# First attention scores of seven batches in 64x32 tiles on TensorE, later due times for weight chunks, and a new order

## The chip, the cores and the metric

The kernel runs on one core of a Trainium2 chip. The core has a matrix engine (TensorE, PE in the profile, with PEld for its weight loads), a vector engine (VectorE, DVE), a scalar engine (ScalarE, ACT), GpSimd (POOL), which here issues the loads, and SyncE (SP), which here issues the stores. The metric is the device time of one execution in microseconds, as the median of several runs.

## The reference

Two stages follow each other. For 8 batches of 8 heads, 576 tokens and head size 64, an attention with 32 packed queries `p` runs in both directions; then a two-layer MLP with squared ReLU is applied to the tokens.

```python
p_packed = sm_attn(p, k, v)            # 32 rows per head: softmax(p k^T / 8) v
out = sm_attn(q, p_packed, p_packed)   # 576 rows per head: softmax(q pp^T / 8) pp
x = out.transpose(0, 2, 1, 3).reshape(4608, 512)
h = x @ w_in                           # 512 x 2048
return (np.maximum(h, 0) ** 2) @ w_out # 2048 x 512
```

## The kernel before

The eight heads of a batch are two quads of four heads; a quad fills 128 partitions (4 heads x 32 dimension pairs of k, or 4 heads x 32 packed queries). Per batch the steps are as follows, with the names that the planner uses.

- **Tk, Tq**: VectorE transposes a quad of k or q (lines 437 and 434) into `kT` and `qT`. The two halves of the head size, `dh` 0 and 1, lie interleaved in the last axis, so that an operand for one half takes every second bf16 element.
- **S1**: the first scores, 128 rows (4 heads x 32 packed queries) by 576 tokens for one quad (line 440, `s1`). The stationary operand `pT_bd` is block-diagonal: 128x128 with one 32x32 block for each head and zeros elsewhere. For each quad there are two matmuls of 512 columns (L446, one for each `dh`) and two of 64 columns (L448), all over the whole 128x128 array, accumulated in a pair of PSUM banks. VectorE takes the row maximum (L452), ScalarE the exponential (L456), after which the pair of banks is free; VectorE normalizes (L462, L463).
- **E, PV, XT**: the probabilities are transposed on TensorE (L469), multiplied with v (L484, column tiles of 64), and the packed outputs are spread out for the next steps (L496).
- **M**: the packed outputs times `w_in`, so that the first MLP layer becomes a product of the second attention's probabilities with a matrix `M` of 128 rows for each quad (L516). These matmuls are 64x32 tiles: eight tiles stand in the array at once. For batch 0 there are eight half steps, one for each quad and each 512-column chunk of `w_in`, for the others two steps of 16 matmuls.
- **S2, C, N**: the second scores (L536, L547, L554), their softmax on VectorE and ScalarE (L566 to L589), and the transposes (L598, L600).
- **F1**: `M` times the probabilities (L613), ReLU on ScalarE (L651), square on VectorE (L661). For batch 0 the tokens are split in a first part FA (256 tokens) and the rest (L626, L635, L642, L644).
- **F2**: the second MLP layer, 16 matmuls of 128x512 for each tile of 128 tokens (L669), the last tile in two halves (L686), then a copy out of PSUM (L356, L358) and the stores.

PSUM has eight banks. Banks 0 to 3 form two pairs (`ps_101`, `ps_102`), used by S1, M, S2 and F1; banks 4 and 5 (`pb_103`, `pb_104`) serve the smaller steps, 6 and 7 (`pb_105`, `pb_106`) F2.

The order of the instructions on every engine is made while the program is built, by a planner (`Plan`). It takes the steps as parallel streams with durations, dependences, due times and PSUM banks, and lets the ready step with the lowest priority value go next; the priorities come from a table of offsets (`TABLE`), one number for each step. A change of the tiling mode on TensorE is charged with `TURN`, 0.098 us in the plan. Loads are issued by GpSimd in the order of their priorities, at most eight at a time; a load counts as landed `LAG` after its own duration. Where the planner sees a gap on TensorE before the first F2 step, it puts in matmuls on zeros (L342) that keep the clock up. On the chip every engine simply executes its own list in order and waits on semaphores.

The lines that matter for what follows are `s1_steps` (one step `S1.b.qd` for each quad, then `E.b.qd`), `tr_steps` (k of the next batch may be transposed once both S1 steps of this batch are done), `load_wi` (the `w_in` chunks), `pv` (which reads the columns of one head in `e1`), and `TABLE`.

Of the kernel before, what the change touches and what calls it, by code (L numbers as in the profile page):

```python
# [8 lines left out]
ACT = mybir.ActivationFunctionType  # L9
# [5 lines left out]
P = 128  # L15
D = 64
NP = 32
QH = 4
JT = 18
GM = 4  # L20
# [33 lines left out]
class Plan:  # L54
# [193 lines left out]
TABLE = {'o': {'P.0': -351.91, 'X.0': -35.89, 'P.2': -372.52, 'X.1': -167.76, 'La0': -651.21, 'La1': -506.79, 'La2':  # L248
# [43 lines left out]


def kernel_impl(tc, q, k, v, p, w_in, w_out, out):
    nc = tc.nc
    B, H, S, Dh = q.shape
    assert Dh == D and S == JT * 32 and H == 2 * QH
    NQD = H // QH
    DMODEL, DFF = w_in.shape
    NE = w_out.shape[1]  # L300
    NFB = DFF // FB
    NWC = DFF // WCH
    HALF = S // 2
    TOK = B * S
    NT = TOK // P
    NKQ, NV, NR = 15, 5, 6
    VX = JT // 2
    TOKH = (2 * P, S - 2 * P)

    with ExitStack() as ctx:  # L310
# [110 lines left out]
        class Att:  # L421
# [53 lines left out]
            def pv(self, qd, u):  # L475
# [3 lines left out]
                for pr in range(2):  # L479
                    c0 = (2 * qd + pr) * NP  # L480
                    for g in range(GM + 1):
                        for e in range(2):
                            h = 2 * pr + e
# [523 lines left out]
```

## Time and profile before

| | us |
|---|---|
| median of 3 runs | 258.02 (257.89 to 258.48) |
| the profiled execution | 258.35 |
| its span | 256.6 |
| PE busy | 246.0 (96%) |
| DVE busy | 174.9 (68%) |
| ACT busy | 166.8 (65%) |
| granted TensorE clock | 1.0 |
| chain that ended last: share of PE | 88% |

The busy time of PE is a union of matmuls that overlap in the pipeline: a single matmul shows its latency (0.38 us for 512 columns), while the next one starts 0.22 us later. What a step costs on a full PE is therefore read as the distance from its first matmul to the first matmul of the step behind it, not as its duration.

### The profile page before, as it was taken

To read this page: it belongs to the slowest core of one execution; us is meant where nothing else is said; L and a number is where in the kernel's file an instruction comes from. 1 tells how busy PE (TensorE), PEld (TensorE's weight loads), DVE (VectorE), ACT (ScalarE), POOL (GpSimd) and SP (SyncE) were. 2 spreads that over 40 slices of the span, in tenths; PEclk is the share of its full clock that TensorE was granted. 3 is DMA by queue.
4 is the path that set the end of the run, shared out by engine and by line. 5 is a ranking of instruction groups with operands and counts; after the bars stand their busy time and mean duration, and the time that the engine had idled before them with its cause. 6 is when DMAs were issued, how large, how long until landed. Compare 5 with 4: busy or idle time off the path is not lost.

```text
span 256.6 us, 5483 instructions
## 1 busy us (share of the span) xinstructions
PE 246.0 (96%) x2142; PEld 143.7 (56%) x2175; DVE 174.9 (68%) x346; ACT 166.8 (65%) x282; POOL 43.3 (17%) x76
## 2 busy tenths in 40 slices
PE   7889999999999999999999999999999999999994
PEld 5556565466545664475446575466544665466542
DVE  7778858877897669966687868567839467657100
ACT  6436999688845796479864477589461685788001
POOL 8745544432424300000000000000000000000000
PEclk9999999999999999999999999999999999999999
DMA  6999999999999999310112020310130211111132
GB/s 112 191 206 204 202 197 209 209 245 233 206 222 228 237 206 191 86 45 0 43 41 74 24 72 0 84 41 0 46 81 19 66 43 31 51 43 39 43 92 74
DMA packets 26617, 28.47 MB, mean 111 GB/s; under 512 B 5472, under 2 KB 18016, under 8 KB 26592
## 3 DMA queue, kind: packets, MB, share of 16 engines
q0 software_dynamic: 18960, 18.55, 44.0%
q1 hardware_dynamic: 7008, 9.38, 13.4%
q8 instruction: 17, 0.28, 0.4%
q10 hardware_dynamic: 624, 0.20, 0.3%
q14 instruction: 8, 0.07, 0.1%
HBM read 37.22 MB, written 9.44 MB: 182 GB/s over the span
## 4 chain that ended last, share of the span: by engine, by line
PE 88%; DVE 6%; issue 1%; ACT 1%; DMA 1%; DVEq 0%; ACTq 0%
PE pb L669 46%; PE ps L613 22%; PE ps L536 3%; PE ps L446 3%; PE pb L484 2%; PE ps L626 2%; PE ps L516 2%; PE pb L516 2%; PE pb L469 1%; PE pb L598 1%; PE pb L686 1%; PE pb L342 1%; DVE M L358 1%; DMA p_f<-in_p_dram 1%; DVE kT L437 1%
## 5 line engine op out<-in xcount | busy, mean ns | idle before, releaser
L669 PE MATMUL pb<-w_out_b,gT 128*128 128x512 bf16 x530 | 139.7, 379 | 1.5 <-issue 0.6
L651 ACT ACTIVATE r<-ps 128x576 bf16<-128x576 f32 x112 | 71.8, 653 | 17.5 <-PE ps L613 13.5
L669 PEld LDWEIGHTS <-gT 128*128 128x128 bf16 x560 | 51.8, 98 | 51.8 <-issue 3.8
L613 PE MATMUL ps<-a,M 128*128 128x288 bf16 x448 | 71.5, 286 | 0.5 <-issue 0.2
L661 DVE TENSOR_TENSOR gT<-r 128x576 bf16<-128x576 bf16 x112 | 50.8, 457 | 29.5 <-ACT r L651 28.8
L613 PEld LDWEIGHTS <-M 128*128 128x128 bf16 x448 | 43.2, 98 | 21.4 <-issue 2.2
L358 DVE COPY o_sb<-pb 128x512 f32<-128x512 f32 (+1 forms) x22 | 14.6, 664 | 13.2 <-PE pb L669 8.7
L456 ACT ACTIVATE e1x<-ps,n 128x576 bf16<-128x576 f32 x16 | 11.8, 739 | 17.1 <-DVE n L452 16.5
L356 ACT COPY o_sb<-pb 128x512 f32<-128x512 f32 (+1 forms) x15 | 8.5, 573 | 19.4 <-PE pb L669 18.2
L356 ACT CAST M<-ps 128x1024 bf16<-128x1024 f32 (+1 forms) x15 | 14.7, 983 | 5.7 <-PE ps L516 5.7
L356 ACT CAST M<-pb 128x512 bf16<-128x512 f32 x29 | 15.9, 599 | 2.4 <-PE pb L516 2.4
L577 ACT ACTIVATE e<-d 128x1152 bf16<-128x1152 f32 (+2 forms) x10 | 9.7, 972 | 8.7 <-DVE d L571 8.6
L342 PE MATMUL pb<-zero 128*128 128x256 bf16 x87 | 13.8, 308 | 1.1 <-DVE zero L361 1.1
L411 POOL DMA_DIRECT2D v_b<-in_v_dram x16 | 11.2, 702 | 13.6 <-DMA k_b<-in_k_dram 8.8
L434 DVE STREAM_TRANSPOSE qT<-q_b 128x576 f32<-128x576 f32 x16 | 11.8, 760 | 1.7 <-DMA q_b<-in_q_dram 1.7
L583 DVE TENSOR_REDUCE t<-e 128x36 f32<-128x1152 bf16 (+2 forms) x10 | 11.0, 1096 | 2.5 <-ACT e L577 2.5
L406 POOL DMA_DIRECT2D q_b<-in_q_dram x16 | 8.9, 562 | 19.9 <-DVE kT L437 7.6
L452 DVE TENSOR_REDUCE n<-ps 128x1 f32<-128x576 f32 x16 | 11.6, 743 | 0.8 <-PE ps L448 0.7
L437 DVE STREAM_TRANSPOSE kT<-k_b 128x576 f32<-128x576 f32 x16 | 11.8, 759 | 0.3 <-DMA k_b<-in_k_dram 0.3
L589 DVE TENSOR_TENSOR n<-e,r 128x1152 bf16<-128x1152 bf16 (+2 forms) x10 | 11.1, 1107 | 0.1
L356 ACT COPY e<-pb 128x640 bf16<-128x640 bf16 x12 | 8.0, 702 | 4.7 <-PE pb L469 4.6
L342 PEld LDWEIGHTS <-zero 128*128 128x128 bf16 x87 | 8.8, 110 | 3.7 <-DVE zero L361 1.1
(75 smaller groups left out, 238.6 us busy)
## 6 DMA issues: line engine op xcount, KB each, us to landing
out_dram<-o_sb SPq DMA_DIRECT2D x140, 64.0 KB, 1.7
k_b<-in_k_dram POOLq DMA_DIRECT2D x16, 288.0 KB, 11.8
q_b<-in_q_dram POOLq DMA_DIRECT2D x16, 288.0 KB, 11.3
v_b<-in_v_dram POOLq DMA_DIRECT2D x8, 320.0 KB, 11.9
v_b<-in_v_dram POOLq DMA_DIRECT2D x8, 256.0 KB, 11.6
w_in_b<-in_moe_w_in_dram POOLq DMA_DIRECT2D x8, 256.0 KB, 10.3
w_out_b<-in_moe_w_out_dram POOLq DMA_DIRECT2D x8, 256.0 KB, 10.3
p_b<-in_p_dram POOLq DMA_DIRECT2D x1, 192.0 KB, 10.6
```

The costliest lines, as they stand in the source:

```text
L342: nc.tensor.matmul(half(7)[:, :2 * P], lhsT=zero[:, :P], rhs=zero, start=True, stop=True)
L356: nc.scalar.copy(dst, src)
L358: eng.tensor_copy(dst, src)
L411: nc.gpsimd.dma_start(self.v[64 * i:64 * i + 64, :, :n * D], src[:, :, i * GM * D:(i * GM + n) * D])
L434: nc.vector.transpose(self.qT[:, qd].rearrange("p s x -> p (s x)").bitcast(F32), self.t.q[qd][:].bitcast(F32))
L437: nc.vector.transpose(kT[:, qd].rearrange("p s x -> p (s x)").bitcast(F32).rearrange("p (x a j2) -> p j2 x a", a=32, j2=2), self.t.k[qd][: ...
L452: nc.vector.tensor_reduce(self.n1[:, qd:qd + 1], self.ps1[qd], axis=AX.X, op=ALU.max, negate=True)
L456: nc.scalar.activation(e1x[:, qd], self.ps1[qd], ACT.Exp, bias=self.n1[:, qd:qd + 1], accum_out=self.d1[:, qd:qd + 1])
L613: nc.tensor.matmul(ps[:, c], lhsT=a.M[:, qd, fb * FB:(fb + 1) * FB], rhs=a.a2[:, qd, c * HALF:(c + 1) * HALF], start=(qd == 0), stop=(qd = ...
L651: nc.scalar.activation(dst, src, ACT.Relu)
L661: eng.tensor_tensor(out=Att.cols(gT[:, fb, o:o + S]), in0=r, in1=r, op=ALU.mult)
L669: nc.tensor.matmul(po[t], lhsT=gT[:, fb, n0:n0 + P], rhs=w_out_b[:, fb, :], start=(fb == 0), stop=(fb == NFB - 1))
```

## The change

In batches 1 to 7 both quads' first scores are computed in one step, `s1_both`, with tiles of 64 rows by 32 columns instead of the whole array. Two heads share a half of the 128 partitions, so a tile takes the 64 partitions of two heads as contraction and the 32 columns of one head of `pT_bd`. Four heads and two quads make eight tiles; to give each its own place in the array, the second quad's heads are stored in the other half of the output partitions (`at`), which `pv` undoes. For each `dh` eight matmuls of 512 columns follow each other, then, for each `dh`, eight of 64 columns: 32 matmuls for a batch instead of 8. Batch 0 stays as it was (`SOLO`).

In the plan the step takes both pairs of PSUM banks at once (`S1.b.0` holds one with no work, `S1.b.1` takes the other and computes). The maximum, exponential and normalization become steps of their own (`SX.b.qd`), each of which frees one pair. The `w_in` chunks 1 to 3 count as landed 1.2 us later than before. All numbers of `TABLE` are new, and with them the order on all engines, loads included.

```diff
+    SOLO = (0,)
...
+            def s1_both(self, u):
+                for qd in range(NQD):
+                    self.ps1[qd] = pair(u[qd]).rearrange("p c n -> p (c n)")[:, :S]
+                for a, z in ((0, GM * P), (GM * P, S)):
+                    for dh in range(2):
+                        for h in range(QH):
+                            for qd in range(NQD):
+                                r, o = slice(h // 2 * 64, h // 2 * 64 + 64), 32 * self.at(qd, h)
+                                dst = self.ps1[qd][o:o + 32, a:z]
+                                if a == 0:
+                                    dst = dst.rearrange("p (g i n) -> p i g n", i=2, n=64)
+                                nc.tensor.matmul(dst, lhsT=pT_bd[r, self.b, qd, dh, 32 * h:32 * h + 32], rhs=kT[r, qd, a:z, dh],
+                                                 start=(dh == 0), stop=(dh == 1))
+
+            def at(self, qd, h):
+                return h ^ 2 if qd and self.b not in SOLO else h
...
-                                             rhs=self.e1[:, qd, g, h * NP:(h + 1) * NP], start=(g == 0), stop=(g == GM))
+                                             rhs=self.e1[:, qd, g, self.at(qd, h) * NP:(self.at(qd, h) + 1) * NP], start=(g == 0), stop=(g == GM))
...
-            return [load_step(f"LWI.{fq}.{cp}", 1.3, lambda cp=cp: dma_w_in(fq, cp), [], 0.71) for cp in range(2)]
+            return [load_step(f"LWI.{fq}.{cp}", 1.3, lambda cp=cp: dma_w_in(fq, cp), [], 0.71, LAG + (1.2 if fq else 0.0)) for cp in range(2)]
...
-                old = [f"S1.{b - 1}.{i}" for i in QDS]
+                old = [f"S1.{b - 1}.{i}" for i in (QDS if b - 1 in SOLO else [1])]
...
+            def hold():
+                n0, nm = f"S1.{b}.0", f"S1.{b}.1"
+                chain = [Step(f"SX.{b}.{qd}", [[[("DVE", 0.67, lambda qd=qd: T[b].s1_max(qd))]], [[("ACT", 0.74, lambda qd=qd: T[b].s1_exp(qd))]],
+                                               [[("DVE", 0.47, lambda qd=qd: T[b].s1_norm(qd))]]], [nm], free=[(1, (n0, nm)[qd])]) for qd in QDS]
+                return [Step(n0, [[[("-", 0.0, lambda: None)]]], [f"Tk.{b}.{qd}" for qd in QDS] + after, banks=HB),
+                        Step(nm, [[[("PE", 0.56, lambda: T[b].s1_both([U[n0], U[nm]]))]]], [n0], banks=HB, mode=2)] + chain
...
-                            [f"S1.{b}.{qd}"], banks=AB, free=[(1, None)])
-            return [one(qd) for qd in QDS] + [two(qd) for qd in QDS]
+                            [f"S1.{b}.{qd}" if b in SOLO else f"SX.{b}.{qd}"], banks=AB, free=[(1, None)])
+            return ([one(qd) for qd in QDS] if b in SOLO else hold()) + [two(qd) for qd in QDS]
```

The order of the loads in the new program begins like the old one (k, v and q of batch 0, then the first two `w_in` chunks, each load in two halves); then it takes the other two `w_in` chunks, k of batch 1, three `w_out` chunks, v of batch 1 and so on, where the old one took k of batch 1, a `w_out` chunk, `w_in` chunk 2, a `w_out` chunk, `w_in` chunk 3, v of batch 1.

More of the change, by code (lines that the diff above doesn't have):

```diff
@@ L245, in use @@
         self.wait, self.margin = z.get("w", 0.0), z.get("m", 0.0)
-TABLE = {'o': {'P.0': -351.91, 'X.0': -35.89, 'P.2': -372.52, 'X.1': -167.76, 'La0': -651.21, 'La1': -506.79, 'La2':
[43 rows of a table removed]
+TABLE = {'o': {'P.0': -301.77, 'X.0': -1069.94, 'P.2': -238.95, 'X.1': -188.5, 'La0': -1231.77, 'La1': -809.34,
[45 rows of a table added]
 def kernel_impl(tc, q, k, v, p, w_in, w_out, out):
@@ L712, in gate, with load_step @@
             return [f1n(y // NFB, y % NFB)] if y >= 0 else []
-        def load_step(name, us, fn, slot=[], issue=0.56):
-            return Step(name, [[[("POOL", issue, fn)]], [[("DMA", us, lambda: None)]]], (), slot + [("dq", 1)], [("dq", 1, None)], lag=LAG0 if name[1:4] in ("k.0", "v.0", "q.0") else LAG)
+        def load_step(name, us, fn, slot=[], issue=0.56, lag=None):
+            return Step(name, [[[("POOL", issue, fn)]], [[("DMA", us, lambda: None)]]], (), slot + [("dq", 1)], [("dq", 1, None)], lag=lag or (LAG0 if name[1:4] in ("k.0", "v.0", "q.0") else LAG))
         def load_kq(b, nm):
@@ L896, in kernel_impl @@
         GATE1 = (-1, -1, -1)
-        SOLO = (0,)
         SPLIT = (0,)
@@ L907, in kernel_impl @@
         NO = [[("-", 0.0, lambda: None)]]
-        plan.levels.update(L=-99, I=-99, LP=-99, I2=5, P=-9, X=-8, G=0, T=0, S1=1, E=1, PV=1, XT=1, S2=2, SB=2.5, SC=2.6, C=2, N=2, M=3, FA=14, F1=15, F2=30)
+        plan.levels.update(L=-99, I=-99, LP=-99, I2=5, P=-9, X=-8, G=0, T=0, S1=1, SX=1, E=1, PV=1, XT=1, S2=2, SB=2.5, SC=2.6, C=2, N=2, M=3, FA=14, F1=15, F2=30)
         plan.stream([Step("P.0", [[[("DVE", 0.2, lambda: nc.vector.tensor_copy(p_b[:, :2 * NQD], p_f))]],
```

88 rows, old and new, of the table TABLE are left out of this document.

## The prediction, made before the changed kernel was run

> **What bounds the kernel now.** I read the first and fourth part of the profile's page, then the busy time by stretches, then the order of time around single steps. The chain that ended last is TensorE for 88% of the span:
>
> ```profile
> PE 246.0 (96%) x2142; PEld 143.7 (56%) x2175; DVE 174.9 (68%) x346; ACT 166.8 (65%) x282; POOL 43.3 (17%) x76
> ...
> PE 88%; DVE 6%; issue 1%; ACT 1%; DMA 1%; DVEq 0%; ACTq 0%
> ```
>
> By stretches (columns: us, then busy time and count of PE, PEld, DVE, ACT, POOL, the granted clock, DMA):
>
> ```profile
> 0.00:12.00 12.00, 9.73 (x83) 6.79 (x83) 8.60 (x24) 6.66 (x12) 9.76 (x23) 1.00 0.95 150
> 12.00:24.00 12.00, 10.63 (x127) 7.71 (x122) 9.01 (x18) 5.24 (x14) 6.05 (x9) 1.00 1.20 204
> 24.00:36.00 12.00, 11.35 (x124) 6.23 (x124) 8.27 (x18) 11.43 (x24) 6.28 (x10) 1.00 1.30 202
> 36.00:100.00 64.00, 63.25 (x582) 36.33 (x591) 51.04 (x101) 49.41 (x79) 21.20 (x36) 1.00 1.22 219
> 100.00:250.00 150.00, 148.35 (x1218) 84.86 (x1238) 98.04 (x187) 93.12 (x156) 0.00 (x0) 1.00 0.19 48
> ```
>
> Two regimes are to be seen. From 36 us on PE is busy 211.6 of 214 us, at full clock, while DVE and ACT have a third free: there the time is the sum of what PE's instructions occupy, and an instruction made shorter is worth its whole saving. Before 36 us PE's 9.7 to 11.4 us of 12 are largely matmuls on zeros; loads, DVE and ACT set the pace.
>
> **The first scores before.** Batch 4's S1, in order of time on PE:
>
> ```profile
> 129.05 0.62 PE L446 MATMUL ps<-kT,pT_bd 128*128 128x512 bf16 x2
> 129.51 0.22 PE L448 MATMUL ps<-kT,pT_bd 128*128 128x64 bf16 x2
> 129.57 0.61 PE L446 MATMUL ps<-kT,pT_bd 128*128 128x512 bf16 x2
> 130.02 0.22 PE L448 MATMUL ps<-kT,pT_bd 128*128 128x64 bf16 x2
> 130.08 0.38 PE L669 MATMUL pb<-w_out_b,gT 128*128 128x512 bf16 x1
> ```
>
> From the first S1 matmul to the F2 matmul behind them: 130.08 - 129.05 = 1.03 us for both quads. Seven batches make 7.21 us, which the change removes.
>
> **The new step.** Nothing in the trace is a 64x32 tile matmul on `kT`, but M has the same tiles, eight in turn, with 512 columns:
>
> ```profile
> 66.78 0.38 PE L669 MATMUL pb<-w_out_b,gT 128*128 128x512 bf16 x1
> 67.09 0.41 PE L516 MATMUL ps<-w_in_b,ppT 64*32 64x512 bf16 x8
> 67.32 0.40 PE L516 MATMUL pb<-w_in_b,ppT 64*32 64x512 bf16 x8
> 67.65 0.39 PE L669 MATMUL pb<-w_out_b,gT 128*128 128x512 bf16 x1
> 67.88 1.06 PE L536 MATMUL ps<-pq_bd,qT 128*128 128x128 bf16 x16
> ```
>
> Eight matmuls last 0.41 us where one lasts 0.38: they run side by side. An F2 matmul in a row of them takes 0.22 us (67.65 to 67.88 is one, to rounding). So 67.09 - 66.78 - 0.22 = 0.09 us is lost on entering the tile mode; the same on leaving, and 67.65 - 67.09 - 0.09 = 0.47 us is what two rounds of eight take. The new step's two 512-column rounds are such rounds: 0.47.
>
> Its two rounds of eight 64-column matmuls have no equal. The nearest are PV's, tiles in turn with 32 columns, and the weight load of M:
>
> ```profile
> 110.67 0.81 PE L484 MATMUL pb<-e,v_b 128*64 128x32 bf16 x40
> 111.41 0.42 PE L613 MATMUL ps<-a,M 128*128 128x288 bf16 x2
> ...
> 67.09 0.14 PEld L516 LDWEIGHTS <-ppT 64*32 64x32 bf16 x16 [0.23 <-issue]
> ...
> L516 PEld LDWEIGHTS <-ppT x256: 88/89/91, 15.3 to 220.5; 64*32 64x32 bf16 x128
> ```
>
> PV's 40 matmuls take 111.41 - 110.67 - 0.09 = 0.65 us, 20 pairs of two tiles, 0.032 each: the lower end for a round. The upper end is a round that waits for a whole weight load: 16 loads take 0.14 us in a row, of which I count the latency of one, 0.09, plus 0.03. Four tiles of 32 columns share 64 rows, twice the loading of a PV pair, so I take 0.06 for a round, 0.12 for both. The step is then 0.47 + 0.12 = 0.59 us, seven times 4.13.
>
> The turns of mode: counted in the order of the two programs, TensorE changes its tiling 76 times before and 86 times after (fewer than 14 more, since the new order also moves M, PV and S2's rest together). 10 x 0.09 = 0.9 us.
>
> Sum on PE: 7.21 - 4.13 - 0.9 = 2.2 us less. With 0.032 for a round it is 2.6, with 0.12 it is 1.3.
>
> One rule of the Trainium skill speaks against the overlap of loads here: "TensorE: Matmul & The Clock Gate", Part 3 (The mechanism), says that a weight load overlaps matmuls in flight only where its row group differs, and eight tiles leave no row group free. By it three later rounds a batch would each wait about 0.09, 1.9 us in all, and the gain would be 0.3; the row above differs, since M's 16 loads all start within 0.05 us of 67.09, while the first eight matmuls run until 67.3.
>
> **Banks.** The step holds both pairs until the exponentials are done, and PE must not need a pair meanwhile. Before, for a batch whose two S1 stood together:
>
> ```profile
> 181.76 0.22 PE L448 MATMUL ps<-kT,pT_bd 128*128 128x64 bf16 x2
> ...
> 181.50 1.42 DVE L452 TENSOR_REDUCE n<-ps 128x1 f32<-128x576 f32 x2 [0.41 <-PE ps L448]
> ...
> 182.30 0.74 ACT L456 ACTIVATE e1x<-ps,n 128x576 bf16<-128x576 f32 x1
> 183.03 0.73 ACT L456 ACTIVATE e1x<-ps,n 128x576 bf16<-128x576 f32 x1
> ...
> 107.46 0.61 PE L598 MATMUL pb<-ident,n 128*128 128x128 bf16 x8
> 107.90 0.22 PE L600 MATMUL pb<-ident,n 128*128 128x128 bf16 x1
> ```
>
> From the start of the maximum the first pair is free after 183.03 - 181.50 = 1.53 us, with the matmul's 0.22 some 1.75 us after the last S1 matmul, the second 0.73 later. In the new order the work between an S1 and the next step that needs a pair is, for batches 2 to 7: 9 F2 + 9 N (2.4 us), S2's rest + 9 F2 (2.2), 9 N + 6 F2 (1.8), 9 F2 (1.9), 15 F2 + 9 N (3.7), XT + 9 F2 (2.1), at 0.22 for an F2 and (107.90 - 107.46)/8 = 0.055 for a transpose of N. All reach 1.75, so I cost it at nothing; if DVE or ACT comes to S1 late, each 0.1 us of that shows on PE in batches 4 and 5 first. The DVE and ACT work itself (maximum, exponential, normalization) is the same in kind and count. `pv` reads other columns at the same cost.
>
> **The start-up.** The new due times and table change the order before 36 us:
>
> ```profile
> 18.68 0.10 PEld L516 LDWEIGHTS <-ppT 64*32 64x32 bf16 x4 [1.23 <-DMA w_in_b<-in_moe_w_in_dram]
> ...
> 20.65 0.39 PE L598 MATMUL pb<-ident,n 128*128 128x128 bf16 x4
> ...
> 21.77 1.09 PE L626 MATMUL pb<-a,M 128*128 128x256 bf16 x8
> ...
> 24.79 0.81 PE L669 MATMUL pb<-w_out_b,gT 128*128 128x512 bf16 x3
> ...
> 26.55 0.62 PE L446 MATMUL ps<-kT,pT_bd 128*128 128x512 bf16 x2
> ...
> 30.65 0.40 PE L516 MATMUL ps<-w_in_b,ppT 64*32 64x512 bf16 x4
> ...
> 22.45 0.58 ACT L635 ACTIVATE r<-pb 128x512 bf16<-128x512 f32 x1
> ```
>
> ```profile
> 11.06 0.54 POOL L406 DMA_DIRECT2D k_b<-in_k_dram  x1 [0.68 <-DMA v_b<-in_v_dram]
> 12.42 0.71 POOL L418 DMA_DIRECT2D w_out_b<-in_moe_w_out_dram  x1 [0.82 <-DMA q_b<-in_q_dram]
> 13.84 0.72 POOL L414 DMA_DIRECT2D w_in_b<-in_moe_w_in_dram  x1 [0.71 <-DMA q_b<-in_q_dram]
> 15.12 0.72 POOL L414 DMA_DIRECT2D w_in_b<-in_moe_w_in_dram  x1 [0.56 <-DMA w_in_b<-in_moe_w_in_dram]
> 16.44 0.72 POOL L418 DMA_DIRECT2D w_out_b<-in_moe_w_out_dram  x1 [0.61 <-DMA w_in_b<-in_moe_w_in_dram]
> ```
>
> ```profile
> w_in_b<-in_moe_w_in_dram POOLq DMA_DIRECT2D x8, 256.0 KB, 10.3
> ```
>
> A load goes out every (16.44 - 11.06)/4 = 1.35 us, because each waits for an older one, and lands 10.3 us later. In the list of loads the last `w_in` half moves from place 18 to 14, k of batch 1 from 11 and 12 to 15 and 16, the first `w_out` from 13 to 17: `w_in` lands 5.4 us earlier, the other two 5.4 us later. What follows on PE: the second M half step of chunk 1 no longer stands ahead of the transposes at 20.65, so these and the first FA matmuls (21.77) come about 0.9 us earlier; the last M half step comes about 5 us earlier than 30.65; the first F2 comes 4 to 5 us later than 24.79, with FA and F1 steps of batch 0 in its place; batch 1's first scores slip from 26.55 to about 29, behind k. What sets the end of this stage is ACT, busy 11.43 of 12 us from 24 to 36; its list in the new order holds the same items (half an M copy more, a copy less), starts the ReLUs about 0.3 us ahead of 22.45, and by my count ends batch 0's at about 39 us as before. So I put the start-up at nothing. Its bounds: the 1.23 us stall and what it delayed gained, -1.2; batch 1 late by its whole 2.4 us with nothing in the gap, +2.4.
>
> **The sum.** The profiled execution took 258.35 us for a span of 256.6, 0.3 above the median of 258.02. 258.35 - 2.2 = 256.2, and beside the median 255.9. I predict 255.9. Its own range, with the rounds' bounds and half a microsecond of start-up either way, is 255.2 to 256.9.
>
> **Rivals.**
> Tile matmuls slowed by their operand, the case on the other side: M's moving operand is contiguous, `kT`'s takes every second element, and four tiles read each half of the partitions at once. If a round of eight then takes twice M's time, the two wide rounds cost 0.47 more a batch, 3.3 in all: 259.2. It decides from 0.31 us a batch on, rounds 1.7 times M's. For it speaks that the old S1 takes 0.23 for a matmul against F2's 0.22; against it, that this is one part in twenty. Chance 0.09.
>
> Rows that exclude each other: both quads' tiles write one bank from both row halves. If the halves took turns, the wide rounds would double, 259.2 too. M does the same (heads of both halves into one quad's bank), and its eight start within 0.03 us. Chance 0.03. (The Trainium skill, "TensorEngine Tiling (Array Packing)", Gotcha 1, says that different row tiles cannot access the same PSUM bank simultaneously; by that rule, this rival. The trace's 0.41 us for eight disagrees as long as the partitions differ.)
>
> Weight loads that do not overlap when all tiles are in use: three rounds a batch wait 0.09 each, 1.9 us of the 2.2 are lost, 257.7. M's loads speak against it, but M never has rounds as short as 64 columns. Chance 0.05.
>
> A start-up that loses: `w_out` and k late, PE waits where F2 used to fill. 1 to 2.4 us take back half to all of the gain, 256.9 to 258.3. It decides where batch 0's last FA/F1 matmuls end after 40 us instead of about 39. Chance 0.17.
>
> A start-up that gains the 1.2 us stall: 254.7. Chance 0.09.
>
> The change does not do what it says, tiles one after another: 16 x 0.22 = 3.5 instead of 0.47, 21 us more, 277. Chance 0.01.
>
> **How the numbers follow.** The forecast has 0.56. A measurement of this kernel tells 0.2% from no change, 0.5 us: faster is below 257.5, slower above 258.5. Faster: 0.56 + 0.09 + half of the losing start-up 0.08 = 0.73. Same: 0.05 + 0.09 = 0.14. Slower: 0.13. The range 254.7 to 258.3 leaves out the tile rivals above (0.13) and a little below.
>
> **What would show it.** Each S1 of batches 1 to 7 as 32 matmuls of 64x32 within about 0.6 us, eight starts within 0.03 us; 0.09 us ahead and behind. PE from 36 us on as full as now. The first FA matmuls near 20.9, the last M half step of batch 0 near 26, and PE's idle time up to 40 us within 1 us of now. Wrong would make it: wide rounds above 0.3 us, 64-column rounds above 0.12, gaps on PE behind S1 that DVE or ACT ends, or F2 matmuls waiting for `w_out` around 30 us.

## The result and the profile after

The changed kernel takes 257.13 us (median of 7 runs, 256.60 to 257.51) against 258.02 (257.79 to 258.48) before: a ratio of 0.9962, 95% interval 0.9949 to 0.9974. A second set of runs gave 257.02 against 258.08 and a ratio of 0.9946 (0.9928 to 0.9963). It is faster, by 0.9 to 1.1 us by the medians and 1.0 to 1.4 by the ratios, where 2.1 were forecast. The profiled execution took 256.86 us, 1.49 less than the profiled one before, for a span of 255.1.

The page of the changed kernel, busy time by engine and the chain that ended last:

```profile
PE 246.8 (97%) x2348; PEld 139.9 (55%) x2348; DVE 172.9 (68%) x339; ACT 168.3 (66%) x289; POOL 43.0 (17%) x76
...
PE 87%; ACT 4%; DMA 3%; DVE 2%; POOL 1%; issue 1%; DVEq 0%; POOLq 0%
```

TensorE is still the bound. By stretches, with the columns of the table before:

```profile
0.00:12.00 12.00, 9.34 (x74) 6.54 (x75) 8.41 (x23) 7.09 (x13) 9.74 (x23) 1.00 0.94 148
12.00:24.00 12.00, 11.29 (x146) 7.53 (x141) 8.90 (x19) 5.56 (x14) 6.05 (x10) 1.00 1.22 204
24.00:36.00 12.00, 11.26 (x138) 7.30 (x137) 7.93 (x16) 12.00 (x26) 5.96 (x10) 1.00 1.25 205
36.00:100.00 64.00, 64.00 (x657) 35.55 (x652) 52.33 (x103) 48.35 (x78) 20.73 (x35) 1.00 1.23 221
100.00:250.00 150.00, 149.94 (x1353) 82.29 (x1352) 95.30 (x180) 94.92 (x163) 0.55 (x1) 1.00 0.19 48
```

From 36 us on PE seems busy for 213.94 of 214 us, with nothing left to lose. That is a trap of this view: a matmul is shown with its latency (0.38 us for 512 columns), and the next one on a full PE starts after 0.22, so a wait of 0.15 us is covered by the latency and counts as busy. The trace before also lacked 33 matmul records (2142 against 2175 weight loads), which lowered its busy time; this one lacks none. What PE loses must be read from distances.

So I did the following with both traces. Each PE instruction gets the distance that it has to its successor in a full row (0.216 us for an F2 matmul, 0.122 for F1, 0.056 for a transpose or an S2 matmul of 128 columns, 0.227 and 0.029 for the old S1 matmuls, 0.0285 for a 512-column tile and 0.0055 for a 64-column one, nothing for the matmuls on zeros, which so count as standing still) and each turn of mode 0.093. Added up in the program's order, these are PE's work; what an instruction starts later than the sum ahead of it is the time that PE has stood still. The split of the span, in us (the parts that wait are good to about 0.1 us, since the distances of the smaller matmuls enter into them):

| kernel | PE's work | still up to 41 us | still after 41 us | last matmul to the end | span |
|---|---|---|---|---|---|
| before | 232.2 | 18.88 | 1.40 | 4.10 | 256.6 |
| before, second profile | 232.2 | 18.90 | 1.39 | 4.10 | 256.6 |
| changed | 229.8 | 18.75 | 2.23 | 4.32 | 255.1 |
| whole array in the new order | 231.9 | 19.81 | 2.05 | 4.33 | 258.1 |
| tiles in the old order | 230.9 | 18.52 | 2.64 | 4.08 | 256.2 |
| the same, E later | 230.9 | 18.72 | 2.33 | 4.09 | 256.1 |
| the same, no first maximum | 230.9 | 18.37 | 1.68 | 4.07 | 255.0 |
| old order, no first maximum | 232.2 | 18.29 | 1.28 | 4.08 | 255.8 |
| old order, later due times | 232.3 | 19.11 | 4.02 | 4.11 | 259.5 |
| new order, waits moved | 229.8 | 18.84 | 1.99 | 4.31 | 254.9 |
| new order, no second maximum, subtraction left out | 229.8 | 18.40 | 4.99 | 4.14 | 257.3 |
| new order, no second maximum, subtraction kept | 229.8 | 18.87 | 2.19 | 4.80 | 255.6 |
| old order, no second maximum | 232.2 | 19.62 | 1.38 | 4.09 | 257.3 |

Before to changed: 2.42 us of PE's work gone (more than the 2.2 forecast), 0.13 less at the start, but 0.83 more standing still after 41 us and 0.22 more at the end: -1.50 in all, the difference of the two spans. The medians of these runs differ by 0.9 only, since the profiled execution before lay 0.3 above its median and this one 0.3 below.

**The step itself** came as forecast. Batch 4's first scores, in order of time:

```profile
124.63 0.59 PE L689 MATMUL pb<-w_out_b,gT 128*128 128x512 bf16 x2
125.15 0.58 PEld L464 LDWEIGHTS <-pT_bd 64*32 64x32 bf16 x32 [0.42 <-issue]
125.15 0.70 PE L464 MATMUL ps<-kT,pT_bd 64*32 64x512 bf16 x32
125.79 2.12 PE L689 MATMUL pb<-w_out_b,gT 128*128 128x512 bf16 x9
```

From its first matmul to the F2 behind it are 125.79 - 125.15 = 0.64 us, 0.55 of it without the turn at its end. The busy time of this line's matmuls in short stretches (us, busy time, and in brackets how many are in flight in the stretch) shows the eights:

```profile
125.15:125.18 0.03, 0.03 (x8) 1.00 0.00 0
125.18:125.38 0.20, 0.20 (x8) 1.00 0.06 10
125.38:125.42 0.04, 0.04 (x16) 1.00 0.00 0
125.42:125.60 0.18, 0.18 (x16) 1.00 0.03 11
125.60:125.64 0.04, 0.04 (x16) 1.00 0.00 0
125.64:125.69 0.05, 0.05 (x24) 1.00 0.00 0
```

Eight matmuls start in the first 0.03 us, none in the next 0.20, eight more at 125.38 to 125.42, and then both 64-column rounds from 125.60 on, within 0.08 us. The weight loads of the same line (PEld) at the start of the step:

```profile
125.14:125.20 0.06, 0.05 (x16) 1.00 0.00 0
```

Sixteen loads, those of the second eight among them, start while the first eight matmuls run until 125.38; the 32 loads lie beside the matmuls and cost nothing. (The Trainium skill, "TensorE: Matmul & The Clock Gate", Part 3 (The mechanism), allows that overlap only where the row group differs, but also says that a load into the background weight buffer is pulled ahead. All row groups are in use here, so the trace disagrees with the first and fits the second, which no run singles out.) The distances are the same to 0.004 us in batches 2 to 7.

**The start** went as forecast too:

```profile
21.52 0.60 PE L646 MATMUL pb<-a,M 128*128 128x256 bf16 x4
...
26.38 0.40 PE L536 MATMUL ps<-w_in_b,ppT 64*32 64x512 bf16 x4
...
28.67 0.38 PE L689 MATMUL pb<-w_out_b,gT 128*128 128x512 bf16 x1
...
29.82 0.77 PE L464 MATMUL ps<-kT,pT_bd 64*32 64x512 bf16 x32
...
39.30 0.41 PE L536 MATMUL ps<-w_in_b,ppT 64*32 64x512 bf16 x8
```

The last M half step of batch 0 (26.38) comes 4.3 us earlier than before, the first F2 (28.67) 3.9 us later, batch 1's first scores (29.82) 3.3 us later, and the time that PE stands still up to 41 us stays what it was.

**What stands still later.** The transposes N of batch 6, on VectorE and TensorE:

```profile
193.08 4.91 PE L689 MATMUL pb<-w_out_b,gT 128*128 128x512 bf16 x22
196.54 1.36 DVE L609 TENSOR_TENSOR n<-e,r 128x1152 bf16<-128x1152 bf16 x1
197.96 0.40 PE L618 MATMUL pb<-ident,n 128*128 128x128 bf16 x4
198.19 0.81 PE L689 MATMUL pb<-w_out_b,gT 128*128 128x512 bf16 x3
198.65 0.30 DVE L361 CAST pq_bd<-pb 32x128 bf16<-32x128 f32 x1
199.00 0.38 PE L618 MATMUL pb<-ident,n 128*128 128x128 bf16 x4
```

22 F2 matmuls take 22 x 0.216 = 4.75 us, so N could start at 197.83; it starts at 197.96, behind the product `n` that ends at 197.90. Three F2 later the second half stands 0.16 us, for the bank that the cast on VectorE leaves at 198.95. Before, no N waited. Added up by the step that stood waiting, the waits after 41 us grew by 0.35 us ahead of N, by 0.2 ahead of F1 in many small pieces, by 0.15 ahead of F2 (nearly all of it at 69.35 us, just behind a copy out of PSUM on VectorE that ends at 69.30) and by 0.13 ahead of M. The one of M is for the pair of banks that the new step holds:

```profile
182.81 1.06 ACT L359 CAST pq_bd<-pb 32x128 bf16<-32x128 f32 x4 [3.21 <-PE pb L516]
183.89 0.74 ACT L476 ACTIVATE e1x<-ps,n 128x576 bf16<-128x576 f32 x1
```

The exponential that frees the pair ends at 184.63, because four casts stand ahead of it on ScalarE, and the M step starts at 184.78, 0.13 us late.

### The profile page after: what moved, and what is told of

Same layout as the page of the kernel before. It is cut to its first block, busy times and chain, and to the rows that moved or that the text cites. A ratio compares the mean times of both kernels' runs of the same rounds, so it can differ in the third digit from the quotient of the medians.

```text
span 255.1 us, 5879 instructions
## 1 busy us (share of the span) xinstructions
PE 246.8 (97%) x2348; PEld 139.9 (55%) x2348; DVE 172.9 (68%) x339; ACT 168.3 (66%) x289; POOL 43.0 (17%) x76
## 4 chain that ended last, share of the span: by engine, by line
PE 87%; ACT 4%; DMA 3%; DVE 2%; POOL 1%; issue 1%; DVEq 0%; POOLq 0%
PE pb L689 46%; PE ps L633 22%; DMA q_b<-in_q_dram 3%; PE ps L556 3%; PE pb L504 2%; PE ps L536 2%; PE ps L464 2%; PE ps L646 2%; PE pb L489 2%; PE pb L618 1%; PE ps L689 1%; PE pb L706 1%; PE pb L536 1%; ACT r L655 1%; ACT gT L662 1%; ACT pq_bd L359 1%
## 5 line engine op out<-in xcount | busy, mean ns | idle before, releaser
L689 PE MATMUL pb<-w_out_b,gT 128*128 128x512 bf16 x544 | 142.9, 380 | 0.0
L359 ACT CAST M<-ps 128x1024 bf16<-128x1024 f32 (+1 forms) x18 | 16.5, 916 | 6.0 <-PE ps L536 5.9
L361 DVE COPY o_sb<-pb 128x512 f32<-128x512 f32 (+1 forms) x20 | 13.2, 662 | 8.5 <-PE pb L706 4.5
L359 ACT COPY o_sb<-pb 128x512 f32<-128x512 f32 (+1 forms) x16 | 9.3, 579 | 14.0 <-PE pb L689 12.8
L359 ACT CAST M<-pb 128x512 bf16<-128x512 f32 x28 | 15.3, 601 | 0.0
L359 ACT COPY a<-pb 128x512 bf16<-128x512 bf16 (+1 forms) x9 | 5.4, 634 | 11.5 <-PE pb L618 10.9
```

The lines of the kernel that those rows point to most:

```text
L359: nc.scalar.copy(dst, src)
L361: eng.tensor_copy(dst, src)
L689: nc.tensor.matmul(po[t], lhsT=gT[:, fb, n0:n0 + P], rhs=w_out_b[:, fb, :], start=(fb == 0), stop=(fb == NFB - 1))
```

## The experiments

My theory: the tiles save on PE what they should, and a part of it comes back, because chains over VectorE and ScalarE keep their length while the work of PE that covers them gets shorter, or lies elsewhere in the new order. The rivals: the tiles save less than their distances say; the new order or its start-up costs by itself; the due times do it.

**The new order without the tiles.** `s1_both` does the eight matmuls of before in the order, the banks and the steps of the changed kernel.

```diff
-                            for qd in range(NQD):
-                                r, o = slice(h // 2 * 64, h // 2 * 64 + 64), 32 * self.at(qd, h)
...
+                for qd in range(NQD):
+                    w = [pT_bd[:, self.b, qd, dh] for dh in range(2)]
+                    main = self.ps1[qd][:, :GM * P].rearrange("p (g i n) -> p i g n", i=2, n=64)
...
+                        nc.tensor.matmul(main, lhsT=w[dh], rhs=kT[:, qd, :GM * P, dh], start=(dh == 0), stop=(dh == 1))
```

> The changed kernel with its order kept on every engine, but the first scores of batches 1 to 7 computed by the old eight matmuls over the whole array, at the place of the tile step. Theory A (the tiles save what PE's rows say, 2.4 us, and the new order loses about 0.9 us in waits for VectorE and at the end that have nothing to do with the tiles): 2.4 us above the changed kernel, about 259.5 us, which is 1.5 us above the kernel before. Theory B (the saving is partly given back because a shorter PE reaches places where VectorE or ScalarE is late; a longer S1 would hide these waits): only 1 to 1.6 us above the changed kernel, 258.1 to 258.7 us. Theory C (the tiles save nothing on the chip in total): as the changed kernel, 257.1 us.

Measured: 258.87 us without one run of 892 us, ratio 1.0040 (1.0019 to 1.0061). The runs lie in two groups, 258.3 to 259.3 (7) and 259.9 to 260.9 (4). The time lies between the forecasts of theories A and B and does not decide; the split does. The profiled run (259.86) is of the upper group, and its PE stood still 1.1 us longer at the start, where k landed late and the clock fell (last section). After that the table shows what matters: of the 0.83 us of new waits 0.65 are there without the tiles (2.05 against 1.40), N of batch 6 waiting 0.13 and 0.16 us and M 0.12 as with them, and so are the 0.22 at the end (4.33). They come with the new order, which alone is slower than before by 0.2% to 0.4% and saves three turns of mode (0.28 us) on PE. The tiles in it save 231.9 - 229.8 = 2.1 us of PE's work and cost 0.18 of new waits; by the medians they are worth 258.87 - 257.02 = 1.9 us, by the lower group's 258.6 it is 1.6.

**The tiles without the new order.** The order, steps and due times of before; in batches 4 to 7, whose two S1 stand together, quad 1's step computes both quads in tiles.

```diff
+    TILED = (4, 5, 6, 7)
...
-                return Step(nm, [[[("PE", 0.49, lambda: T[b].s1(qd, U[nm]))]], [[("DVE", 0.67, lambda: T[b].s1_max(qd))]],
+                return Step(nm, [[[("PE", 0.49, lambda: (T[b].s1_tiles if b in TILED else T[b].s1)(qd, U[nm]))]], [[("DVE", 0.67, lambda: T[b].s1_max(qd))]],
```

> The kernel before with its order kept on every engine; in batches 4 to 7, where its two S1 steps stand directly behind each other, their eight matmuls are replaced by the 32 tile matmuls. Theory A: each of the four batches saves 1.03 - 0.73 = 0.30 us, 1.2 us in all, about 256.8 us. Theory B: half of it, 257.4 us. Theory C: 258.0 us.

Measured: 258.04, ratio 0.9994 (0.9982 to 1.0006): nothing gained. PE's work is 1.26 us shorter, and PE stands still 1.24 us longer after 41 us. The largest new wait, in batch 7:

```profile
180.28 0.80 PE L463 MATMUL ps<-kT,pT_bd 64*32 64x512 bf16 x32
181.13 2.11 PE L688 MATMUL pb<-w_out_b,gT 128*128 128x512 bf16 x9
181.20 1.42 DVE L471 TENSOR_REDUCE n<-ps 128x1 f32<-128x576 f32 x2 [0.71 <-PE ps L463]
183.05 0.37 DVE L482 TENSOR_SCALAR e1n<-e1x,r 128x576 bf16<-128x576 bf16 x1
183.48 0.45 PE L488 MATMUL pb<-ident,e1n 128*128 128x128 bf16 x5 [0.24 <-DVE e1n L482]
```

The transposes E follow the scores after a softmax of one quad: from the first maximum (181.20) to the end of `e1n` (183.42) 2.2 us. PE has the four XT and nine F2 in between, 9 x 0.216 = 1.94 us from 181.13, and waits 0.40 at 183.48. Before, with the scores in the whole array, the same nine F2 stood there:

```profile
180.79 0.61 PE L446 MATMUL ps<-kT,pT_bd 128*128 128x512 bf16 x2 [0.16 <-issue]
...
181.93 2.11 PE L669 MATMUL pb<-w_out_b,gT 128*128 128x512 bf16 x9
...
183.36 0.37 DVE L463 TENSOR_SCALAR e1n<-e1x,r 128x576 bf16<-128x576 bf16 x1
...
183.88 0.44 PE L469 MATMUL pb<-ident,e1n 128*128 128x128 bf16 x5
```

But quad 0's maximum (181.50, 0.71 us after the first scores; here 0.92 after) could start while PE was still at quad 1's scores. The tiles finish both quads together, so quad 0's chain starts later within the step, and PE is through sooner. From the first score on, cover and chain were 3.08 and 2.94 us before (183.87 and 183.73, less 180.79); now they are 2.79 and 3.14. Two such waits ahead of E (0.33 and 0.40 us) and two behind them (M 0.13, F1 0.16) make 1.0 of the 1.24 us.

**Due times alone.** The kernel before with the later due times of the `w_in` chunks, and its old table.

```diff
-            return [load_step(f"LWI.{fq}.{cp}", 1.3, lambda cp=cp: dma_w_in(fq, cp), [], 0.71) for cp in range(2)]
+            return [load_step(f"LWI.{fq}.{cp}", 1.3, lambda cp=cp: dma_w_in(fq, cp), [], 0.71, LAG + (1.2 if fq else 0.0)) for cp in range(2)]
```

> The kernel before, with the later due time of the weight chunks in the plan alone, the old table and the old S1. If the due time is what makes the start-up better, PE's idle time up to 36 us is below the 18.7 us of before, by up to 1 us, and the time 257.0 to 258.0 us. If a due time only helps with a table made for it, the order is worse: 258 to 261 us.

Measured: 261.21, ratio 1.0114 (1.0086 to 1.0142). The old table of offsets was made for other due times, and with these the order gets worse. PE's waits from 30 to 62 us in this kernel, by what they waited for (us in total, times, longest):

```profile
PE ps L516 <- ACT e1x L456: 1.7, 2, 1.4
```

M waits for a pair of banks that the exponentials of S1 still hold; before had no such wait. By itself the later due time brings nothing; what it is worth with the new table, no run shows.

**The changed kernel again**, for a second profile.

> The changed kernel once more, for a second profile. If the 1.5 us between the two profiled executions are the typical difference, the span is again near 255.1 us; if the profile shown was a lucky one, it is 255.4 to 255.7 us, and the additional time shows as gaps on PE after 36 us. Time 257.1 us.

Measured: 257.02, ratio 0.9946 (0.9928 to 0.9963). The span is 255.2 us, near the first profile's 255.1, which was no lucky one. The waits of the first profile are there again, to some 0.01 us each: they belong to the order and are no scatter. Only at the start does this one stand still 0.15 us longer (18.9 us).

**The waits moved.** In the changed kernel the steps N.6.0, N.6.1, M.6.0 and N.4.0 are put behind one more F2 matmul each on PE; nothing else changes.

```diff
+DELAY = {'N.6.0': 1, 'N.6.1': 1, 'M.6.0': 1, 'N.4.0': 1}
...
-        for p in sorted(out, key=lambda p: p.start):
+        for p in self.late(sorted(out, key=lambda p: p.start)):
```

> The changed kernel, in which four steps that PE waited for in both profiles are issued one F2 matmul (0.22 us) later: both transposes of batch 6's second probabilities (waits 0.13 and 0.16 us), the first M step of batch 6 (0.13) and the first transposes of batch 4's (0.05). Theory A (such waits are what the new order loses; they are local, and an F2 matmul put ahead removes them): 0.4 us below the changed kernel, 256.6 us, and PE's idle time after 41 us 1.8 instead of 2.2 us. Theory D (PE waits there because it is ahead of the other engines, so a wait removed in one place comes up at the next): no change, 257.0 us, and the same 2.2 us.

Measured: 256.69 (256.46 to 257.18), ratio 0.9931 (0.9908 to 0.9955), the best kernel of the study that computes everything. Batch 6's N:

```profile
196.52 1.36 DVE L625 TENSOR_TENSOR n<-e,r 128x1152 bf16<-128x1152 bf16 x1
198.02 0.39 PE L634 MATMUL pb<-ident,n 128*128 128x128 bf16 x4
...
198.98 0.38 PE L634 MATMUL pb<-ident,n 128*128 128x128 bf16 x4
```

The product ends at 197.88, and N comes at 198.02 with an F2 in the place of the wait; the second N starts 0.96 us after the first, where it was 1.04. Four moved steps make 0.24 us less standing still after 41 us and 0.3 to 0.4 less by the medians. At the moved steps 0.40 us of waits go, and 0.16 come back ahead of F1, which now waits for the copies of the moved transposes by ScalarE (0.07 us at 141.77 and 0.08 at 200.20). The other waits ahead of F1 stay (many of some 0.02 us, more than half of their time just behind the end of a ReLU).

**The tiles in the old order, E later.** As above, with E.5.0, E.7.0, PV.5.0 and F1.5.0 behind two more F2 matmuls and M.5.2 behind one.

```diff
+DELAY = {'PV.5.0': 2, 'E.5.0': 2, 'E.7.0': 2, 'F1.5.0': 2, 'M.5.2': 1}
```

> The kernel before with tiles in batches 4 to 7, as in the run that gained nothing, but with the steps that waited there issued one or two F2 matmuls later: the transposes E of batches 5 and 7 (waits 0.33 and 0.40 us) and PV of batch 5 by two, M of batch 5 and the F1 behind it (0.13 and 0.16) by one and two. Theory B (the tiles' saving was given back because the softmax of the first scores, of a fixed length, was covered by PE work that has become shorter): these waits go, 0.8 to 1.0 us below that run, 257.1 us. Theory D (PE is ahead of the others as a whole): 257.8 to 258.0 us, with the waits in other places.

Measured: 257.84, ratio 0.9993 (0.9970 to 1.0015), the same as without the moves (0.9994). Theory B's 257.1 did not come; the time is that of theory D, with waits in other places. PE stands still 0.3 us less after 41 us than there, and 0.9 more than before: the wait ahead of quad 0's transposes in batch 7 is gone, but 0.42 us now stand ahead of quad 1's at 184.31, whose softmax ends 0.7 us behind quad 0's, at 184.05; the last release that the profile names there is that of three casts on ScalarE, at 184.26. A moved step does not help where the next one waits for a chain too.

**The scores' chain made shorter.** The test of the theory in the old order: the row maximum of the first softmax is left out in batches 4 to 7 (the exponential takes a bias of zero), so that its chain is 0.7 us shorter for a quad, while PE, ScalarE and the order stay. Once with the tiles and once, as a control, in the kernel before.

```diff
-                nc.vector.tensor_reduce(self.n1[:, qd:qd + 1], self.ps1[qd], axis=AX.X, op=ALU.max, negate=True)
+                if self.b < 4:
+                    nc.vector.tensor_reduce(self.n1[:, qd:qd + 1], self.ps1[qd], axis=AX.X, op=ALU.max, negate=True)
...
-                nc.scalar.activation(e1x[:, qd], self.ps1[qd], ACT.Exp, bias=self.n1[:, qd:qd + 1],
+                nc.scalar.activation(e1x[:, qd], self.ps1[qd], ACT.Exp, bias=self.n1[:, qd:qd + 1] if self.b < 4 else zero[:].bitcast(F32)[:, :1],
```

> Tiles in batches 4 to 7 in the order of before, without the row maximum of the first softmax in those batches: the chain from the scores to the transposes of E is 0.71 us shorter for each quad. Theory A (the tiles' gain of 1.26 us came back as waits for this chain, which the tiles don't shorten): the waits ahead of E (0.72 us) and of the M steps (0.3 us) go and the gain shows, 257.0 to 257.3. Theory B (it came back in the tiles themselves or in the start-up): 257.8 to 258.1.

> The control: the kernel before without the row maximum of the first softmax in batches 4 to 7. Its trace has no wait ahead of E above 0.1 us, so both theories expect 258.0 to 258.3, idle time of PE after 41 us 1.3 to 1.4.

Measured: 256.94 (256.81 to 257.27), ratio 0.9929 (0.9907 to 0.9951) with the tiles; 257.97, ratio 0.9987 (0.9966 to 1.0007) without. The tiles that gained nothing (258.04) now gain 1.0 us over the control. PE with tiles and the short chain:

```profile
180.43 2.11 PE L689 MATMUL pb<-w_out_b,gT 128*128 128x512 bf16 x9
182.38 0.44 PE L489 MATMUL pb<-ident,e1n 128*128 128x128 bf16 x5
182.87 0.59 PE L689 MATMUL pb<-w_out_b,gT 128*128 128x512 bf16 x2
183.30 0.44 PE L489 MATMUL pb<-ident,e1n 128*128 128x128 bf16 x5
```

E follows its nine F2 at once (180.43 + 9 x 0.216 = 182.37). PE's standing still after 41 us fell from 2.64 to 1.68 us, in the control from 1.40 to 1.28. So it is shown that in the old order the tiles' gain was held back by the chain behind the scores.

**The second softmax made shorter, first try.** The changed kernel without the maximum of the second softmax in batches 1 to 7 and without its subtraction: the exponential reads the scores where they stand.

```diff
             def s2_exp(self, x):
...
+                if self.b not in SOLO:
+                    for y in (3, 2):
+                        g0, g1 = self.GR[y]
+                        nc.scalar.activation(self.e2[:, g0:g1], self.src2(y), ACT.Exp, scale=0.125)
+                    return
```

> The changed kernel without the maximum and its subtraction in the second softmax of batches 1 to 7 (the exponential reads the scores from PSUM): 2.5 us less on VectorE for a batch, one more ScalarE instruction. Nothing of PE's list changes. Theory A (the waits in the new order are for a VectorE that is late by some 0.1 us): the waits ahead of N go, 0.4 to 0.7 us below the changed kernel, 256.3 to 256.6 us. Theory D': they are for ScalarE or for PSUM; no change, 257.0 us.

Measured: 259.30, ratio 1.0044 (1.0024 to 1.0063), 2.2 us slower than the changed kernel, though VectorE has 18 us less to do. One of three waits that make it, in this kernel:

```profile
90.43 1.02 ACT L603 ACTIVATE e<-ps 128x1024 bf16<-128x1024 f32 x1
...
91.50 0.65 PE L642 MATMUL ps<-a,M 128*128 128x288 bf16 x4 [0.85 <-ACT e L603]
```

and the same place in the changed kernel:

```profile
88.28 1.22 DVE L591 TENSOR_TENSOR d<-ps,m 128x1024 f32<-128x1024 f32 x1
```

There the subtraction empties the pair of banks by 89.50. Without it the exponential does so, at its place in ScalarE's list, by 91.45, and the F1 behind it waits 1.0 us by its distance; two M steps wait 0.8 and 1.0 us in the same manner. My edit had moved the release of the banks, so the run does not answer its question; it does show what holding a pair for 2 us more costs.

**The same, with the subtraction kept** (of zero), so that the banks are freed as before; and the same edit in the kernel before as a control.

```diff
+                if self.b:
+                    return
                 nc.vector.tensor_reduce(self.m2[:, g0:g1], self.src2(x), axis=AX.X, op=ALU.max)
...
-                                        in1=self.m2[:, g0:g1].unsqueeze(2).to_broadcast([P, g1 - g0, 32]), op=ALU.subtract)
+                                        in1=(zero[:].bitcast(F32) if self.b else self.m2)[:, g0:g1].unsqueeze(2).to_broadcast([P, g1 - g0, 32]), op=ALU.subtract)
```

> The changed kernel without the row maximum of the second softmax in batches 1 to 7 (the subtraction stays, of zero, so that VectorE frees the PSUM banks as before): the order on every engine is that of the changed kernel, and each batch's second softmax is ready about 1.5 us earlier (the maximum's 1.23 + 0.28 us). Theory A (after 41 us PE stands still because chains behind it, above all the second softmax, have a fixed length and the new order leaves them too little cover): the waits ahead of the transposes of N (0.34 us) go, idle time of PE after 41 us falls from 2.23 to 1.8 or less, time 256.6 or less. Theory B (those waits are PE's own, of issue and weight loads): 257.0, idle as it was.

> The control: the kernel before without the row maximum of the second softmax in batches 1 to 7, in the order of before. It has no wait ahead of N (0.00 us) in its trace, so both theories expect nothing to gain after 41 us: 258.0 to 258.2, idle time of PE after 41 us 1.3 to 1.4. If it gains 0.4 or more, the maximum costs something in any order, and the run beside it shows nothing about the new order.

Measured: 257.37, ratio 0.9940 (0.9917 to 0.9964) in the new order, no clear difference from the changed kernel (0.9962 and 0.9946); 258.36, ratio 0.9993 (0.9971 to 1.0014) in the old one. Theory A's 256.6 did not come: the waits ahead of N stay, but for 0.06 us. Batch 6 in the new order without the maximum:

```profile
192.85 0.28 DVE L593 TENSOR_TENSOR d<-pb,zero 128x128 f32<-128x128 f32 x1
...
193.17 1.16 ACT L599 ACTIVATE e<-d 128x1152 bf16<-128x1152 f32 x1 [3.03 <-DVE d L593]
...
196.62 1.36 DVE L611 TENSOR_TENSOR n<-e,r 128x1152 bf16<-128x1152 bf16 x1
...
198.03 0.40 PE L620 MATMUL pb<-ident,n 128*128 128x128 bf16 x4
```

The exponential takes all 1152 columns at once and waits for the last 128 of them, from S2's rest, which PE computes only at 192.4, behind PV. The large maximum, done long before, was not in the chain; of the chain, which takes 5.6 us from S2's rest to N in both kernels, only 0.3 us went, most of it lost again at the sum, which has three casts ahead of it on VectorE; and the second half waits for the same bank as before. It is a chain of fixed length that holds up N, as the theory has it, but I had named the wrong link, and a direct test with that chain shortened was not made; for N it rests on the moved steps.

**Before again**, for the scatter of a profile.

> The kernel before once more, for a second profile. Theory A: PE's idle time up to 41 us is 18.4 to 18.9 us and after 41 us 1.4 us again, its span 256.2 to 256.6 us.

Measured: 258.56, ratio 1.0013 (0.9994 to 1.0032) to other runs of the same kernel. The split is that of the first profile, to 0.02 us in each part, so the differences between the rows of the table after 41 us are differences of the kernels. That holds although k landed later here: the first scores of batch 0 started at 7.45 and 9.24 us, against 7.17 and 8.20. Nothing of it is left at the half step of M at 18.69 (18.68 in the first profile): there it had waited 1.23 us for `w_in`, and that wait is gone here.

## Why the prediction was right and wrong

- The step: 0.59 us forecast, 0.55 measured. The wide rounds were right (0.23 each); the 64-column rounds take 0.04 each where 0.06 was taken. All three rivals on the tiles (slowed by a strided operand, taking turns at a bank, waiting for weight loads) are out: eight start within 0.03 us, and the loads lie beside the matmuls. (The rule on banks of "TensorEngine Tiling (Array Packing)", Gotcha 1, of the Trainium skill would have the two row halves take turns at a quad's bank; the eight starts disagree where, as here, the partitions differ.)
- The turns: ten more at 0.09 us, as counted (13 by the tiles, three fewer by the new order).
- The sum on PE: 2.2 forecast, 2.42 by the distances. Right.
- The start-up at nothing: right, 18.75 against 18.88 us of standing still, with the steps at the places that were forecast, the first FA matmuls excepted (21.52 where 20.9 was expected, and no gain from it).
- Banks at nothing: nearly. The condition named for a cost (ScalarE late at the exponentials) came true once, at XT and 9 F2 of batch 7 and not in batches 4 and 5 as expected, for 0.13 us.
- What failed is the first step: "there the time is the sum of what PE's instructions occupy, and an instruction made shorter is worth its whole saving". It made the forecast treat every other wait of the new order as nothing without looking at one. The waits grew by 0.83 us after 41 us, and the end by 0.22, so that 2.42 - 0.83 - 0.22 + 0.13 = 1.50 remain between the two profiled executions. So the term that was wrong is that of the waits behind 36 us, put at nothing. The sentence rested on busy time and its 211.6 of 214 us, which cannot show waits that a matmul's latency covers. The experiment with the tiles in the old order is the plain counterexample: 1.26 us less work, 1.24 more waiting, no gain.
- Which part brought the loss: the new order's own waits make 0.65 of the 0.83, without any tile. The 0.22 at the end are there without the tiles too, but not in every kernel of the new order (4.14 us without the second maximum and subtraction, where before had 4.10). That the old order would have done better is no answer, since with tiles in four batches it gains nothing; in the new order most of the tiles' saving comes through. The causes of the small new waits ahead of F1 stay open.
- So the split turns the 2.2 us forecast into 1.5 between the first two profiles (1.4 between the second two). Down to the 0.9 to 1.1 of the medians 0.3 to 0.6 us more are missing. The sum set the profile of before 0.3 above its median and assumed the same after; the profiled execution after lay 0.3 below, the second one at its median. In the table the time still up to 41 us goes from 18.3 to 18.9 us between profiles with nearly the same order at the start (those at 19.6 and 19.8 and the later due times left aside), so single executions scatter there by as much; more than that is not settled.

## What to carry to other kernels

When an engine looks full, add up the distances of its instructions and compare with their starts: the waits hide in the latency that a busy share counts as work. An instruction made shorter on the bounding engine also shortens the cover of every chain that runs beside it, so look at each consumer behind the changed step, how much work stands between, and how long its chain is, and expect the whole saving only where there is slack. With an order fixed at build time, one repair to try is to put one more piece of ready work ahead of the consumer that waits; here it gained 0.3 to 0.4 us in the new order and nothing in the old one.

## What the hardware showed beside this

In the profile of the new order with whole-array scores, k landed late and PE had no matmul for 2.0 us at the start. Columns: us, busy times, and the third number from the right is the granted clock.

```profile
7.00:8.50 1.50, 1.24 (x6) 0.63 (x6) 0.82 (x3) 0.00 (x0) 1.50 (x3) 0.59 1.37 188
8.50:10.00 1.50, 1.50 (x8) 0.64 (x7) 1.07 (x2) 0.39 (x1) 1.50 (x3) 0.50 1.35 209
10.00:12.00 2.00, 2.00 (x20) 1.66 (x18) 1.36 (x5) 1.27 (x4) 1.08 (x2) 0.83 1.13 212
```

```profile
7.26 1.01 PE L449 MATMUL ps<-kT,pT_bd 128*128 128x512 bf16 x2 [2.04 <-DVE kT L440]
```

From about 7.3 us on the clock was half for some 3.4 us, and PE stood still 1.1 us longer by 41 us; how much of that is the clock and how much the late k is not separated. A late k alone cost nothing in the second profile of before, but there it only took the place of a wait of 1.23 us for `w_in`; the changed kernel has no such wait at that step (19.17 us), and here the step comes 1.15 us later (20.32). In the other profiles the clock stayed at 1.00 at the start, with a gap of 0.90 us in the changed kernel and of up to 1.82 in others (the old order without the first maximum). Where between 1.82 and 2.04 us the clock gives way, or whether the gap alone decides, one instance does not say.

The end of the changed kernel is 0.22 us longer than before although its last steps are the same. Its last two stores are issued here:

```profile
251.46 0.83 ACTq L700 DMA_DIRECT2D out_dram<-o_sb  x2
```

0.71 us after the last matmul's start at 250.75; before it was 253.18 - 252.47 = 0.71 too. What differs is the time to the landing of the last store, 3.6 us after the issue against 3.4; of the other kernels in the new order one has 4.1 (without the second maximum) and one 3.4 (without its subtraction as well). Why is open.
